# Gated recurrence and cosine MLP on one core: the evictions of a two-bank PSUM tile by two engines, without a wait between them

## The chip, the cores and the metric

The kernel runs on one core of a Trainium2 chip. A core has a matrix engine (TensorE: PE for the multiplications, PEld for its weight loads), three engines for elementwise work (VectorE or DVE, ScalarE or ACT, GpSimd or POOL), a sequencer that mostly issues DMAs (SyncE or SP), a memory of 128 partitions (SBUF), and an accumulator memory that TensorE writes (PSUM, eight banks for each partition; a bank holds 512 float32 values). Every engine works through its own queue of instructions in order; engines wait for one another by semaphores. The metric is the device time of one execution in microseconds (us), as the median of several runs.

## The reference

```
# q, k, v, alpha: (B, H, S, D) = (4, 8, 768, 48)
state = zeros(B, H, D, D)
for t in range(S):
    state = alpha[:, :, t, :, None] * state + einsum('bhd,bhe->bhde', k[:, :, t], v[:, :, t])
    y[:, :, t] = einsum('bhd,bhde->bhe', q[:, :, t], state)

x = y.transpose(0, 2, 1, 3).reshape(B * S, H * D)     # 3072 x 384
h = x @ w_in                                          # 384 -> 2048
out = (h * cos(h)) @ w_out                            # 2048 -> 384
```

A linear-attention recurrence with a decay for each channel is followed by an MLP whose activation is h cos(h). Inputs and output are float32.

## The kernel before

The 3072 tokens are cut into twelve steps J = 0 to 11, three for each batch entry; a step holds 256 tokens of all 8 heads, as two chunks c = 0 and 1 of 128 tokens. For each step the recurrence is computed in chunked form:

- `load` brings a (alpha), k, q and v into SBUF through SP's queue. `ln` takes the logarithm of a on ACT, `cums` sums it along the tokens by matmuls, `icp` and `exps` (on ACT) make the inverse and the plain cumulative products, and `scale_k` and `scale_q` (L212, L216; on POOL or DVE) multiply k and q by them into kh and qh. From J = 3 on POOL first multiplies pairs of a (`mul_a`, L149).
- `trans` (L260): 64 small transposes by PE write T_ps, a PSUM tile of two banks, one for each chunk c. `evict_T` (L266) copies bank c into half c of the SBUF tile qkT.
- `scores` (L274) computes A_ps of a chunk from qkT, `mask` (L279, DVE) masks it into A_sb.
- `outer` (L291) computes the chunk's state update U_ps; `add_state` (L305, L307, DVE) and `decay_state` (L313, POOL) carry the state un on.
- `yT` (L340) computes the recurrence's output y_ps, again a PSUM tile of two banks, one for each chunk. `evict_y` (L351) casts bank c into half c of the SBUF tile xT.
- The MLP: `mlp1` (L361) makes h_ps in four parts u, `cosine` (L367, ACT) makes c_sb, `gate` (L372, DVE) multiplies both into gsb, `mlp2` (L390, L384 for the last tile) makes o_ps in four parts for each chunk, `evict_o` (L402, L398) copies it out, `store` (L408) issues the DMA to HBM.

PSUM's eight banks are shared out: three two-bank buffers with the tag "h" go round among T_ps, A_ps, U_ps, y_ps, h_ps and a few smaller uses in the order in which they are asked for, one bank goes to o_ps, one to the cumulative sums. So whoever asks for an "h" buffer waits until the tile that used it three requests earlier has been read.

The order of all work is written out by hand: the table PLAN gives each step (such as `evT 0` of J = 3) a number, the steps are recorded in the order of these numbers, and each engine runs its share in that order. The numbers set an order only. A letter behind a number picks the engine: evictions of T go to DVE unless `:A` (ACT) stands there, evictions of y go to ACT unless `:D` (DVE) stands there. The rows that matter here:

```
"evT 0": "14773:A 18473:A 41585 48048 60976 71899 81566:A 93894 111044 116949:A 129834 138061",
"evT 1": "16453:A 19403:A 43330 48048:A 59896 72979 81586 93289 112124 117657 128759 137201:A",
"evy 0": "21333:D 27535:D 49128:D 60501:D 73683 92814:D 91919 110094:D 125423 140998 152879:D 163777:D",
"evy 1": "21333 27658 48990 59421:D 73683:D 92339:D 91549 110569:D 125793 141368 152128 163814",
```

The two halves of one tile are on different engines for T of J = 3, 6, 9 and 11 and for y of J = 0, 1, 2, 4, 10 and 11: ten pairs. The framework that places the waits treats the two-bank PSUM tile as one thing that two engines access, and makes the eviction that is recorded second wait for the first, although each reads a bank of its own and writes a half of its own. Whoever needs both halves then waits for the second alone.

Two more places are touched without a change in order: the last matmul of `yT` of J = 1 is remembered (GATES, AFTER), and the loads of a from J = 2 on, in SP's order, stand behind it; and `mlp2` counts which of its four parts is the first and the last of a tile.

Of the kernel before, what the change touches and what calls it, by code (L numbers as in the profile page):

```python
# [9 lines left out]
FP = mybir.dt.float32  # L10
# [6 lines left out]
def kernel(  # L17
# [10 lines left out]
    nc = tc.nc  # L28
    B, H, S, D = q.shape
    DM, DF = moe_w_in.shape  # L30
    C = 128
# [17 lines left out]
    ps = ctx.enter_context(tc.tile_pool(name="ps", bufs=1, space=bass.MemoryType.PSUM))  # L49
# [14 lines left out]
    for c in range(2):  # L64
        r = slice(HC * c, HC * c + HC)
# [105 lines left out]
    def two_banks(name):  # L171
        return ps.tile([C, 2, 512], FP, tag="h", name=name, bufs=3)
# [76 lines left out]
        )  # L249

    T_ps, A_ps, y_ps, U_ps = {}, {}, {}, {}

    def trans(J):
        T_ps[J] = ps.tile([C, 2, 2 * NP, 2, HC], BF, tag="h", name="T_ps", bufs=3)
        for i, x in ((1, kh_t[J % NQ]), (0, qh_t[J % NQ])):
            for p in range(NP):
                for e in range(2):
                    for c in range(2):
                        r = slice(HC * c, HC * c + HC)
                        nc.tensor.transpose(T_ps[J][:, c, i * NP + p, e, :],  # L260
                                            x[r, e, 2 * p : 2 * p + 2, :].rearrange("s h d -> s (h d)"), ident_bf[r, r])

    def evict_T(J, c, copy):
        if J not in qkT_sb:
            qkT_sb[J] = sb.tile([C, 2, 2 * NP, C], BF, tag="qkT", name="qkT", bufs=BUF["qkT"])
        copy(out=qkT_sb[J][:, c], in_=T_ps[J][:, c].rearrange("r n e s -> r n (e s)"))  # L266

    def scores(J, c):
        qkT = qkT_sb[J]
        A_ps[J, c] = ps.tile([C, 2, NP, C], FP, tag="h", name="A_ps", bufs=3)  # L270
        for p in range(NP):
            for a in range(2):
                r = slice(64 * a, 64 * a + D)
                nc.tensor.matmul(A_ps[J, c][:, a, p, :], qkT[r, c, NP + p, :], qkT[r, c, p, :], start=True, stop=True)  # L274

    def mask(J, c):
        if J not in A_sb:
# [39 lines left out]
    def yT(J):  # L317
        y_ps[J] = two_banks("y_ps")
        qkT, A, vs = qkT_sb.pop(J), A_sb.pop(J), vs_t[J % NS]
        todo = []  # L320
        for i in range(KT):
            for c in range(2):
                for g in range(4):
                    p, x = (4 * i + g) // 3, (4 * i + g) % 3
                    if (2 * J + c) % (2 * NJB) > 0:
                        U = U_new[2 * J + c - 1].rearrange("r p a d -> r p (a d)")
                        todo.append((c, g, i, U[:, p, 32 * x : 32 * x + 32], qkT[:, c, p, :]))
        for i in range(KT):
            for c in range(2):
                vf = vs[:, c].rearrange("s h d -> s (h d)")  # L330
                for half in range(2):
                    for g in range(4):
                        p, x = (4 * i + g) // 3, (4 * i + g) % 3
                        parts = {0: [(0, 0)], 1: [(0, 32), (1, 48)], 2: [(1, 80)]}[x]
                        for a, d in parts[half : half + 1]:
                            todo.append((c, g, i, vf[:, 128 * p + d : 128 * p + d + 32], A[:, c, a, p, :]))
        outs = [m[:3] for m in todo]
        begun = set()
        for z, (c, g, i, l, r) in enumerate(todo):
            last = nc.tensor.matmul(y_ps[J][32 * g : 32 * g + 32, c, i * C : (i + 1) * C], l, r,  # L340
                             start=(c, g) not in begun, stop=(c, g, i) not in outs[z + 1 :], skip_group_check=True)
            begun.add((c, g))
        for key, step in GATES.items():
            if step == ("yT", J):
                AFTER[key] = last

    def evict_y(J, c, copy):
        if J not in xT:
            xT[J] = sb.tile([C, KT, T2], BF, tag="xT", name="xT", bufs=BUF["xT"])

        copy(out=xT[J][:, :, c * C : (c + 1) * C].rearrange("r i (t e) -> r i e t", e=2),  # L351
             in_=y_ps[J][:, c, 0 : KT * C].rearrange("r (i e t) -> r i e t", i=KT, e=2))

    h_ps, c_sb, o_ps, o_sb = {}, {}, {}, {}

# [18 lines left out]

    HALVES = [slice(0, DM // 2), slice(DM // 2, DM)]

    def mlp2(J, c, part):
        if (J, c) == (NJ - 1, 1):
            if part == 0:

                o_ps[J, c] = [ps.tile([C, 512], FP, tag="x", name="o_last", bufs=1), two_banks("o_last")[:, 0]]
            for z, cols in enumerate(HALVES):
                for ft in range(part * NF // MP, (part + 1) * NF // MP):
                    nc.tensor.matmul(o_ps[J, c][z][:, 0 : DM // 2], gsb[J][:, ft, c * C : (c + 1) * C], w2[:, ft, cols],  # L384
                                     start=(ft == 0), stop=(ft == NF - 1))
            return
        if part == 0:
            o_ps[J, c] = ps.tile([C, 512], FP, tag="o", name="o_ps", bufs=1)
        for ft in range(part * NF // MP, (part + 1) * NF // MP):
            nc.tensor.matmul(o_ps[J, c][:, 0:DM], gsb[J][:, ft, c * C : (c + 1) * C], w2[:, ft],  # L390
                             start=(ft == 0), stop=(ft == NF - 1))

    def evict_o(J, c, copy):
        if (J, c) == (NJ - 1, 1):
            o_sb[J, c] = []
            for z, cp in enumerate((nc.scalar.copy, nc.vector.tensor_copy)):
                t = sb.tile([C, DM // 2], FP, tag=f"o_half{z}", name="o_half", bufs=1)
                cp(out=t, in_=o_ps[J, c][z][:, 0 : DM // 2])  # L398
                o_sb[J, c].append((t, HALVES[z], (nc.scalar, nc.sync)[z]))
        else:  # L400
            t = sb.tile([C, DM], FP, tag="o_sb", name="o_sb", bufs=4)
            copy(out=t, in_=o_ps.pop((J, c))[:, 0:DM])  # L402
            o_sb[J, c] = [(t, slice(0, DM), nc.sync)]

    def store(J, c):
# [6 lines left out]
    def idle(n):  # L412
# [132 lines left out]
```

## Time and profile before

| | |
|---|---|
| runs | 188.44 us median of 3 (188.35 to 189.09) |
| profiled execution: span from its first to its last instruction | 186.5 us |
| its own time | not given on the page; the median run lies 1.9 us over this span |
| PE busy | 176.7 us, 95% of the span |
| DVE, ACT, POOL busy | 135.4, 126.5 and 77.1 us |
| granted TensorE clock | 1.000 |
| input loads (k, a, v, q) | 12 of each, 384 KB each, a median of 6.0 to 6.3 us from issue to landing |
| HBM | read 25.17 MB, written 4.72 MB |

The profile is one execution, seen instruction by instruction. A row of the timeline has the start from the span's begin, the length, the engine, the line of the kernel, the operation with its output and inputs, the shapes, a count, and in brackets the idle time of the engine ahead of it with what ended it. Busy time is an average over stages: in the first 110 us the loads of q, k, v and a run beside the compute, after that nearly none. The list of waits sums, for each pair of waiter and releaser, the time in which an engine stood idle. Consecutive rows of one engine may overlap by some 0.1 us, since the next operation starts while the last one drains.

### The profile page before, as it was taken

To read this page: it belongs to the slowest core of one execution; us is meant where nothing else is said; L and a number is where in the kernel's file an instruction comes from. 1 tells how busy PE (TensorE), PEld (TensorE's weight loads), DVE (VectorE), ACT (ScalarE), POOL (GpSimd) and SP (SyncE) were. 2 spreads that over 40 slices of the span, in tenths; PEclk is the share of its full clock that TensorE was granted. 3 is DMA by queue.
4 is the path that set the end of the run, shared out by engine and by line. 5 is a ranking of instruction groups with operands and counts; after the bars stand their busy time and mean duration, and the time that the engine had idled before them with its cause. 6 is when DMAs were issued, how large, how long until landed. Compare 5 with 4: busy or idle time off the path is not lost.

```text
span 186.5 us, 5746 instructions
## 1 busy us (share of the span) xinstructions
PE 176.7 (95%) x2467; PEld 126.4 (68%) x2469; DVE 135.4 (73%) x184; ACT 126.5 (68%) x161; POOL 77.1 (41%) x110
## 2 busy tenths in 40 slices
PE   7988799989989999999999999999999999999993
PEld 2434588655667786785688668676867686786872
DVE  7178775589799979698847987794977556754461
ACT  2466876889498986889668999728965264373330
POOL 5079510257645653781896076930360320100000
PEclk9999999999999999999999999999999999999999
DMA  6999999999949979996799932600041005301102
GB/s 152 261 258 165 181 204 237 259 266 265 274 105 304 264 180 245 264 260 167 186 278 278 247 104 46 182 0 4 4 136 47 5 0 158 118 0 66 64 0 84
DMA packets 60137, 29.47 MB, mean 158 GB/s; under 512 B 51024, under 2 KB 60112, under 8 KB 60112
## 3 DMA queue, kind: packets, MB, share of 16 engines
q1 hardware_dynamic: 56256, 25.86, 57.2%
q0 software_dynamic: 3712, 3.15, 11.0%
q8 instruction: 19, 0.31, 0.7%
q10 hardware_dynamic: 144, 0.10, 0.2%
q14 instruction: 6, 0.05, 0.1%
HBM read 25.17 MB, written 4.72 MB: 160 GB/s over the span
## 4 chain that ended last, share of the span: by engine, by line
PE 73%; ACT 15%; DVE 8%; issue 3%; DVEq 0%
PE h_ps L361 31%; PE o_ps L390 24%; PE idle_ps L416 4%; PE y_ps L340 3%; ACT qkT L266 3%; DVE gsb L372 3%; PE T_ps L260 2%; ACT c_sb L367 2%; PE A_ps L274 2%; ACT L136 2%; ACT cp L200 2%; PE U_ps L291 2%; DVE kh L212 2%; ACT icp L192 2%; PE o_last L384 1%
## 5 line engine op out<-in xcount | busy, mean ns | idle before, releaser
L372 DVE TENSOR_TENSOR gsb<-h_ps,c_sb 128x1024 bf16<-128x1024 f32 x48 | 58.1, 1221 | 21.9 <-ACT c_sb L367 21.2
L367 ACT ACTIVATE c_sb<-h_ps,halfpi 128x1024 bf16<-128x1024 f32 x48 | 53.0, 1113 | 26.8 <-PE h_ps L361 23.0
L361 PE MATMUL h_ps<-xT,w 128*128 128x256 bf16 x576 | 66.7, 273 | 1.3 <-ACT xT L351 0.7
L390 PE MATMUL o_ps<-w,gsb 128*128 128x384 bf16 x368 | 66.7, 327 | 0.1
L361 PEld LDWEIGHTS <-w 128*128 128x128 bf16 x576 | 55.6, 98 | 10.1 <-issue 1.6
L390 PEld LDWEIGHTS <-gsb 128*128 128x128 bf16 x368 | 33.8, 98 | 21.2 <-DVE gsb L372 0.6
L313 POOL TENSOR_TENSOR un<-us,c 128x384 bf16<-128x384 f32 x20 | 16.7, 835 | 40.7 <-DVE us L305 29.1
L279 DVE TENSOR_TENSOR A_sb<-A_ps,msk 128x1024 bf16<-128x1024 f32 x24 | 28.9, 1215 | 1.7 <-PE A_ps L274 1.7
L212 POOL TENSOR_TENSOR kh<-k,icp 128x384 bf16<-128x384 f32 x17 | 16.9, 999 | 9.2 <-ACT icp L192 7.8
L216 POOL TENSOR_TENSOR qh<-q,cp 128x384 bf16<-128x384 f32 x15 | 15.0, 1006 | 11.8 <-ACT cp L200 11.8
L149 POOL TENSOR_TENSOR a<-a 128x384 f32<-128x384 f32 x9 | 9.0, 1001 | 12.6 <-DMA a<-in_alpha_dram 12.6
L219 POOL CAST vp<-v 128x768 bf16<-128x768 f32 x12 | 10.1, 841 | 8.8 <-DMA v<-in_v_dram 7.7
L416 PE MATMUL idle_ps<-zeros 128*128 128x512 bf16 x38 | 12.0, 457 | 1.4 <-DVE zeros L52 1.2
L141 ACT ACTIVATE lna<-a 128x768 bf16<-128x768 f32 x12 | 10.2, 847 | 4.6 <-DMA a<-in_alpha_dram 4.6
L266 ACT COPY qkT<-T_ps 128x1024 bf16<-128x1024 bf16 x8 | 8.0, 1015 | 6.9 <-PE T_ps L260 4.4
L136 ACT ACT_TABLE_LOAD x9 | 11.5, 1283 | 0.9 <-PEq L529 0.7
L367 ACT ACT_TABLE_LOAD x9 | 11.5, 1283 | 0.2
L266 DVE COPY qkT<-T_ps 128x1024 bf16<-128x1024 bf16 x16 | 10.8, 678 | 1.1 <-ACT qkT L266 1.1
L305 DVE TENSOR_TENSOR us<-U_ps,un 128x384 f32<-128x384 f32 x16 | 8.7, 550 | 3.8 <-PE U_ps L291 2.8
L402 DVE COPY o_sb<-o_ps 128x384 f32<-128x384 f32 x12 | 6.6, 551 | 6.5 <-PE o_ps L390 6.5
L351 ACT CAST xT<-y_ps 128x384 bf16<-128x384 f32 x12 | 6.7, 594 | 5.6 <-PE y_ps L340 3.8
L351 DVE CAST xT<-y_ps 128x384 bf16<-128x384 f32 x12 | 6.8, 584 | 4.7 <-PE y_ps L340 2.9
(69 smaller groups left out, 159.1 us busy)
## 6 DMA issues: line engine op xcount, KB each, us to landing
k<-in_k_dram SPq DMA_DIRECT2D x12, 384.0 KB, 6.0
a<-in_alpha_dram SPq DMA_DIRECT2D x12, 384.0 KB, 6.1
v<-in_v_dram SPq DMA_DIRECT2D x12, 384.0 KB, 6.0
q<-in_q_dram SPq DMA_DIRECT2D x12, 384.0 KB, 6.3
out_dram<-o_sb SPq DMA_DIRECT2D x23, 192.0 KB, 2.6
vs<-vp SPq DMA_DIRECT2D x36, 64.0 KB, 2.1
w<-in_moe_w_out_dram POOLq DMA_DIRECT2D x4, 384.0 KB, 10.1
w<-in_moe_w_in_dram POOLq DMA_DIRECT2D x4, 384.0 KB, 7.3
```

The costliest lines, as they stand in the source:

```text
L136: nc.scalar.preload_act_table_set("natural_log_exp_and_others")
L212: eng.tensor_tensor(out=kh_t[J % NQ][:, e, :, 0:D], in0=kqv["k", J][:, :, e], in1=icp_, op=ALU.mult)
L216: eng.tensor_tensor(out=qh_t[J % NQ][:, e, :, 0:D], in0=kqv["q", J][:, :, e], in1=cp, op=ALU.mult)
L266: copy(out=qkT_sb[J][:, c], in_=T_ps[J][:, c].rearrange("r n e s -> r n (e s)"))
L279: nc.vector.tensor_tensor(out=A_sb[J][:, c].rearrange("s a p t -> s (a p) t"), in0=A_ps.pop((J, c)).rearrange("s a p t -> s (a p) t"), in1 ...
L313: nc.gpsimd.tensor_tensor(out=u, in0=U_sum.pop(n), in1=c2_sb[J][:, :, c].unsqueeze(3).to_broadcast([C, NP, 2, D]), op=ALU.mult)
L351: copy(out=xT[J][:, :, c * C : (c + 1) * C].rearrange("r i (t e) -> r i e t", e=2), in_=y_ps[J][:, c, 0 : KT * C].rearrange("r (i e t) -> ...
L361: nc.tensor.matmul(h_ps[J, u][:, f, :], w1[:, kk, ft * C : (ft + 1) * C], xT[J][:, kk, :], start=(kk == 0), stop=(kk == KT - 1))
L367: nc.scalar.activation(out=c_sb[J, u], in_=h_ps[J, u], func=AF.Sin, bias=halfpi, scale=1.0)
L372: nc.vector.tensor_tensor(out=gsb[J][:, u * FW : (u + 1) * FW], in0=h_ps.pop((J, u)), in1=c_sb.pop((J, u)), op=ALU.mult)
L390: nc.tensor.matmul(o_ps[J, c][:, 0:DM], gsb[J][:, ft, c * C : (c + 1) * C], w2[:, ft], start=(ft == 0), stop=(ft == NF - 1))
L416: nc.tensor.matmul(idle_ps[0], zeros[:, 0:C], zeros, start=True, stop=True)
```

## The change

The two evictions of a tile are declared independent where they are on different engines. `apart` remembers the last eviction of each tile and its engine; if the next one of the same tile is on another engine, it tells the framework that there is no dependency between the two. The dependencies of both on the matmuls that write the tile, and of later users on both, are kept. PLAN is as it was. The rest of the diff rearranges code: the remembering of a step's last matmul becomes a function (`pass_gate`) that `scores` calls too, with no gate set there, and `mlp2` counts its parts instead of going by their number; neither moves an instruction.

```diff
+    evicts = {}
+
+    def apart(key, copy, ins):
+        if key in evicts and evicts[key][0] != copy:
+            tc.declare_no_dep(ins.ins, evicts[key][1].ins, reason="two engines each evict a bank of their own")
+        evicts[key] = copy, ins
...
     def evict_T(J, c, copy):
...
-        copy(out=qkT_sb[J][:, c], in_=T_ps[J][:, c].rearrange("r n e s -> r n (e s)"))
+        ins = copy(out=qkT_sb[J][:, c], in_=T_ps[J][:, c].rearrange("r n e s -> r n (e s)"))
+        apart(("T", J), copy, ins)
...
     def evict_y(J, c, copy):
...
-        copy(out=xT[J][:, :, c * C : (c + 1) * C].rearrange("r i (t e) -> r i e t", e=2),
+        ins = copy(out=xT[J][:, :, c * C : (c + 1) * C].rearrange("r i (t e) -> r i e t", e=2),
              in_=y_ps[J][:, c, 0 : KT * C].rearrange("r (i e t) -> r i e t", i=KT, e=2))
+        apart(("y", J), copy, ins)
...
+    def pass_gate(step, last):
+        for key, gate in GATES.items():
+            if gate == step:
+                AFTER[key] = last
...
-        for key, step in GATES.items():
-            if step == ("yT", J):
-                AFTER[key] = last
+        pass_gate(("yT", J), last)
...
+        last_tile = (J, c) == (NJ - 1, 1)
+        done = parts_done[J, c] = parts_done.get((J, c), 0) + 1
+        if done == 1:
...
+                nc.tensor.matmul(o[:, 0 : cols.stop - cols.start], gsb[J][:, ft, c * C : (c + 1) * C], w2[:, ft, cols],
+                                 start=(done == 1 and ft == fts[0]), stop=(done == MP and ft == fts[-1]))
```

More of the change, by code (lines that the diff above doesn't have):

```diff
@@ L259, in trans @@
                         r = slice(HC * c, HC * c + HC)
-                        nc.tensor.transpose(T_ps[J][:, c, i * NP + p, e, :],
+                        last = nc.tensor.transpose(T_ps[J][:, c, i * NP + p, e, :],
                                             x[r, e, 2 * p : 2 * p + 2, :].rearrange("s h d -> s (h d)"), ident_bf[r, r])
@@ L273, in scores @@
                 r = slice(64 * a, 64 * a + D)
-                nc.tensor.matmul(A_ps[J, c][:, a, p, :], qkT[r, c, NP + p, :], qkT[r, c, p, :], start=True, stop=True)
+                last = nc.tensor.matmul(A_ps[J, c][:, a, p, :], qkT[r, c, NP + p, :], qkT[r, c, p, :], start=True, stop=True)
+        pass_gate(("scores", J, c), last)
     def mask(J, c):
@@ L375 @@
     HALVES = [slice(0, DM // 2), slice(DM // 2, DM)]
+    parts_done = {}
     def mlp2(J, c, part):
-        if (J, c) == (NJ - 1, 1):
-            if part == 0:
+        last_tile = (J, c) == (NJ - 1, 1)
+        done = parts_done[J, c] = parts_done.get((J, c), 0) + 1
+        if done == 1:
+            if last_tile:
                 o_ps[J, c] = [ps.tile([C, 512], FP, tag="x", name="o_last", bufs=1), two_banks("o_last")[:, 0]]
[L382 to L391, printed above, removed]
+            else:
+                o_ps[J, c] = [ps.tile([C, 512], FP, tag="o", name="o_ps", bufs=1)]
+        fts = range(part * NF // MP, (part + 1) * NF // MP)
+        for o, cols in zip(o_ps[J, c], HALVES if last_tile else [slice(0, DM)]):
+            for ft in fts:
+                nc.tensor.matmul(o[:, 0 : cols.stop - cols.start], gsb[J][:, ft, c * C : (c + 1) * C], w2[:, ft, cols],
+                                 start=(done == 1 and ft == fts[0]), stop=(done == MP and ft == fts[-1]))
     def evict_o(J, c, copy):
@@ L401, in evict_o @@
             t = sb.tile([C, DM], FP, tag="o_sb", name="o_sb", bufs=4)
-            copy(out=t, in_=o_ps.pop((J, c))[:, 0:DM])
+            copy(out=t, in_=o_ps.pop((J, c))[0][:, 0:DM])
             o_sb[J, c] = [(t, slice(0, DM), nc.sync)]
```

## The prediction

> **What bounds the kernel now.** I read the page's busy shares first, then the list of waits, then the timeline around every place where TensorE stood still.
>
> The busy shares, part 1 of the page:
>
> ```profile
> PE 176.7 (95%) x2467; PEld 126.4 (68%) x2469; DVE 135.4 (73%) x184; ACT 126.5 (68%) x161; POOL 77.1 (41%) x110
> ```
>
> PE is busy 176.7 of 186.5 us, so a gain can come only out of PE's standing time. The granted clock is 1.000 over the span. Going through the timeline of PE, the gaps after its first 21 us are 0.65 us (ending 22.20), 0.26 (27.44), 0.61 (41.66), 0.11 (49.15), 0.59 (52.07), 0.26 (77.09), 0.35 (86.94), 0.12 (99.39) and 0.30 (120.06): 3.25 us in all. The list of waits (who waited for whom: us in total, times, longest) shows the waits that the change is about:
>
> ```profile
> ACT qkT L266 <- DVE qkT L266: 2.4, 1, 2.4
> ACT xT L351 <- DVE xT L351: 1.8, 3, 0.8
> DVE xT L351 <- ACT xT L351: 1.8, 2, 1.1
> DVE qkT L266 <- ACT qkT L266: 1.1, 2, 0.9
> PE h_ps L361 <- ACT xT L351: 0.7, 1, 0.7
> PE U_ps L291 <- DVE xT L351: 0.6, 1, 0.6
> PE U_ps L291 <- DVE gsb L372: 0.4, 1, 0.4
> PE h_ps L361 <- DVE xT L351: 0.3, 1, 0.3
> ```
>
> The first four are one eviction waiting for the other of its pair: 7.1 us over eight pairs. The last four are PE's own, and each follows one of those. The timeline (start, length, in brackets the idle time before) joins them, place by place:
>
> ```profile
> 20.94 0.59 DVE L351 CAST xT<-y_ps 128x384 bf16<-128x384 f32 x1
> 21.56 0.59 ACT L351 CAST xT<-y_ps 128x384 bf16<-128x384 f32 x1 [0.83 <-DVE xT L351]
> 22.20 4.09 PE L361 MATMUL h_ps<-xT,w 128*128 128x256 bf16 x36 [0.65 <-ACT xT L351]
> 27.44 1.47 PE L361 MATMUL h_ps<-xT,w 128*128 128x256 bf16 x12 [0.26 <-DVE gsb L372]
> ...
> 49.17 0.68 DVE L266 COPY qkT<-T_ps 128x1024 bf16<-128x1024 bf16 x1
> 49.88 1.01 ACT L266 COPY qkT<-T_ps 128x1024 bf16<-128x1024 bf16 x1 [2.40 <-DVE qkT L266]
> 50.79 0.60 ACT L351 CAST xT<-y_ps 128x384 bf16<-128x384 f32 x1
> 51.42 0.59 DVE L351 CAST xT<-y_ps 128x384 bf16<-128x384 f32 x1 [1.11 <-ACT xT L351]
> 52.07 0.51 PE L291 MATMUL U_ps<-vp,kh 64*128 64x96 bf16 x16 [0.59 <-DVE xT L351]
> ...
> 76.45 0.59 DVE L351 CAST xT<-y_ps 128x384 bf16<-128x384 f32 x1 [0.66 <-ACT xT L351]
> ...
> 85.07 0.69 DVE L266 COPY qkT<-T_ps 128x1024 bf16<-128x1024 bf16 x1 [0.90 <-ACT qkT L266]
> ```
>
> **The change, part by part.** Set side by side, the two programs have the same compute and DMA instructions in the same order on all engines. What differs is waits: ten pairs split over two engines (y of J = 0, 1, 2, 4, 10, 11; T of J = 3, 6, 9, 11) lose the wait for each other, and whoever needed only the later of the two now waits for both. PE gets two more waiting instructions and ACT one.
>
> *y of J=0 (22 us).* ACT is free from 20.74 (its vs copy, 19.92 + 0.82), y_ps is complete at 20.88, so the ACT half runs at 20.9 to 21.5, beside DVE's, and PE's h_ps starts at 21.6 to 21.7 instead of 22.20. Late next: DVE. c_sb would end 24.3 instead of 24.82, but DVE's us (24.04, waiting for POOL) ends 24.60, and DVE's next operation starts some 0.08 before the end of the one ahead, as 27.31 after 27.39 does. So the first gsb runs 24.52 to 25.74, the second 25.66 to 26.89 (it ended 27.39), and it frees the buffer of the h_ps that now starts 26.93 instead of 27.44. Gain 0.51, taken as 0.50; bounds 0.3 (only the move of the first gsb, 24.86 to 24.52) and 0.61 (all that PE gets at 22.20).
>
> *y of J=1.* PE has other h_ps work until 29.2 and the later half ends 28.51: nothing. If that cover were gone, ACT's idle 0.47.
>
> *T of J=3 and y of J=2 (49 to 52 us).* T_ps is written at 48.87 (48.47 + 0.40); ACT has been idle since 47.5, so its qkT half runs at 48.9 to 49.9. y_ps is complete at 50.06: ACT's xT half runs 50.1 to 50.7, DVE's after its cp (49.77 + 0.55) at 50.3 to 50.9. Scores and o_ps keep PE until 51.48, and U_ps, which waited for y_ps's buffer, starts there: 0.59 gained, all of the gap. Late next: the mask of A_ps, which frees the next h_ps buffer; it moves from 51.90 to 50.9 and stays ahead. Bounds 0.4 and 0.59.
>
> *y of J=4 (77 us).* DVE's half can start at 75.8 (its qkT ends 75.78, y_ps is complete at 75.74), ACT's ends 76.42, both ahead of PE's free time at 76.83: 0.26 gained.
>
> *T of J=6 (87 us).* DVE's qkT half starts at 84.1 (its gsb ends 84.17, T_ps is written at 83.98) and not 85.07, so the gsb behind it ends some 0.8 earlier than 86.89 and PE's 0.35 before U_ps goes.
>
> *T of J=9, 11, y of J=10, 11.* PE runs without a gap behind each of them (120.06 to the end), the engines' own idle time there is 0.18, 0, 0 and 0.48: nothing. They would be worth that much if PE were not the bound.
>
> *Costs.* A waiting instruction is 51 ns on PE's load side (the one row at L361); two, and ACT's, make at most 0.12; they stand where PE waits or has work queued: 0. In four places a weight load now carries a wait that only its matmul had; a load is 98 ns, and in none of them is the wait the last to end: 0, at most 0.4.
> Two evictions of one tile at the same time are not in this trace. Nearest rows: DVE's 16 qkT copies take 659 to 692 ns and ACT's 8 take 1012 to 1032, whatever ran beside them; ACT's copy at 140.49 took 1.01 while DVE's A_sb, from 140.72, read other PSUM. I take 0; the other end, one after the other as now, takes the whole gain away.
>
> *Sum:* 0.50 + 0.59 + 0.26 + 0.35 = 1.70 us off the span of 186.5. The runs' median is 188.44, 1.9 over that span, so I take the profiled execution as a median one and leave the 1.9: 186.7. The gains add up, because the gaps that stay between the places move with them: at 41.66 PE waits for DVE's qh, DVE (its kh at 39.16) for ACT's icp, ACT (37.88) for PE's cums; at 49.15 for POOL's un behind that same DVE; at 120.06 for DVE's gsb behind ACT's c_sb, which waited for PE (101.55). Between them PE has no gap, and a of J=2, which cums needs, lands at 34.3 for its use at 35.96, so 0.5 fits.
>
> **The rivals.**
> *More: a collision dissolves (186.1).* DVE's products of two SBUF tiles take 0.55 alone, but the second qh of J=2 took 1.35 (40.25 to 41.60), beside POOL's product on a (40.16 to 41.18, released by a load), and PE's 0.61 gap at 41.66 waits for it. DVE arrives 0.5 earlier at 39.74; POOL's load, behind a gate in yT of J=1 that moves by some 0.4, lands for 39.74 too. If DVE is first, the product is 0.55 and the gap goes: 1.70 + 0.61 = 2.31.
> [...]
>
> *Less: loads hold the first stage (187.2).* a of J=4 lands at 40.1 and v of J=2 at 41.6, both used within 0.1; if they don't move, the first 0.50 is lost. Against it: their queue is fed behind the gate that moves.
>
> *None: ACT holds (188.4).* From 102.9 to 119.6 ACT runs without a gap (table loads, c_sb, exponentials). If its start there didn't follow PE, the whole 1.70 would vanish in front of it. Against it: its c_sb at 98.65 and 101.55 each waited 0.20 for PE.
>
> *The waits remain by another way (188.4):* through a buffer's release or an engine's order. Against it: the wait lists name PE where they named the other evictor.
>
> *Slower: more collisions (190.4).* Seven DVE products (39.16 to 68.2 us: 0.69, 0.55, 1.35, 1.27, 0.55, 0.55, 0.79) would cost 3.70 more if every one met POOL and took 1.35; DVE is busy 11.15 of 11.40 us from 39.0 to 50.4, so it would pass to PE: 188.44 - 1.70 + 3.70. It decides from 2.64 us on (1.70 plus the 0.94 of 0.5%). Against it: POOL's work there waits on the same chain and moves with it.
>
> **How the numbers follow.** Forecast 0.50; more 0.18; loads 0.14; ACT 0.10; waits remain 0.04; slower 0.04. About 0.5% (0.94 us) is what a measurement of this kernel can tell from no change. Faster: 0.50 + 0.18 + 0.14 = 0.82; same 0.10 + 0.04 = 0.14; slower 0.04. The range runs from the larger gain (186.1, a little under for its 0.1 bounds) through 187.2 with the lower bounds 0.3 and 0.4 at their places and the uncovered 0.4 of weight loads: 186.0 to 187.8. It leaves out 0.18.
>
> **What would show it.** The list of waits no longer has any of its first four lines above. PE's gaps ending 22.20, 52.07, 77.09 and 86.94 are gone, with PE's gap near 27 at about 0.16; U_ps of J=3 stands 1.1 earlier, the T_ps at 120.06 stands 1.70 earlier, and PE's busy time stays 176.7. The forecast is wrong if evictions side by side take over 0.7 (DVE) or 1.05 (ACT), if the gap before T_ps at 41.66 closes or grows, or if a new PE gap stands between 27 and 49 or 102 and 120.

## The result and the profile after

The changed kernel takes 186.47 us (median of 4 runs, 185.82 to 186.89), the kernel before beside it on the same chip 188.45 us (188.35 to 189.09). The ratio is 0.9887 (95% interval 0.9859 to 0.9915): 1.6 to 2.7 us faster, most likely 2.0 to 2.1. The forecast was 186.7 us, 1.74 below the median of before.

The busy shares of the changed kernel:

```profile
PE 175.6 (95%) x2469; PEld 125.7 (68%) x2469; DVE 134.7 (73%) x184; ACT 126.4 (69%) x161; POOL 77.3 (42%) x110
```

The span went from 186.5 to 184.0 us in the profiled runs, with PE still 95% busy. (The profiled run of the changed kernel is its fastest, 185.82 us; what the run itself adds to the difference is told below.) The list of waits (waiter, line, releaser: us in total, times, longest) no longer holds any of the four lines in which one eviction waits for the other. In after, `evict_T` is L278, `evict_y` L363, `outer` L305, `mlp1` L374, `gate` L385. What evictions wait for now is PE, and PE's own waits have other names:

```profile
ACT qkT L278 <- PE T_ps L272: 5.8, 4, 2.2
ACT xT L363 <- PE y_ps L354: 4.0, 5, 1.6
DVE xT L363 <- PE y_ps L354: 3.2, 3, 2.3
PE cums L160 <- ACT lna L146: 0.4, 1, 0.4
PE T_ps L272 <- DVE gsb L385: 0.3, 1, 0.3
PE h_ps L374 <- DVE us L319: 0.3, 1, 0.3
PE U_ps L305 <- POOL un L327: 0.2, 1, 0.2
```

The timeline of the changed kernel at the four places of the forecast (start, length, engine, line, operation; in brackets the idle time before):

```profile
20.98 0.59 ACT L363 CAST xT<-y_ps 128x384 bf16<-128x384 f32 x1 [0.20 <-PE y_ps L354]
20.98 0.59 DVE L363 CAST xT<-y_ps 128x384 bf16<-128x384 f32 x1
21.72 2.78 PE L374 MATMUL h_ps<-xT,w 128*128 128x256 bf16 x24
23.23 0.83 POOL L327 TENSOR_TENSOR un<-us,c 128x384 bf16<-128x384 f32 x1 [2.00 <-DVE us L319]
24.09 0.56 DVE L319 TENSOR_TENSOR us<-U_ps,un 128x384 f32<-128x384 f32 x1 [0.95 <-POOL un L327]
24.79 1.47 PE L374 MATMUL h_ps<-xT,w 128*128 128x256 bf16 x12 [0.29 <-DVE us L319]
27.09 1.16 PE L374 MATMUL h_ps<-xT,w 128*128 128x256 bf16 x9
...
48.57 1.01 ACT L278 COPY qkT<-T_ps 128x1024 bf16<-128x1024 bf16 x1 [1.43 <-PE T_ps L272]
48.63 0.67 DVE L278 COPY qkT<-T_ps 128x1024 bf16<-128x1024 bf16 x1
49.59 0.59 ACT L363 CAST xT<-y_ps 128x384 bf16<-128x384 f32 x1
49.69 0.57 DVE L363 CAST xT<-y_ps 128x384 bf16<-128x384 f32 x1
50.77 0.51 PE L305 MATMUL U_ps<-vp,kh 64*128 64x96 bf16 x16
...
74.56 0.60 ACT L363 CAST xT<-y_ps 128x384 bf16<-128x384 f32 x1
74.56 0.59 DVE L363 CAST xT<-y_ps 128x384 bf16<-128x384 f32 x1
75.41 1.47 PE L374 MATMUL h_ps<-xT,w 128*128 128x256 bf16 x12
...
82.34 1.01 ACT L278 COPY qkT<-T_ps 128x1024 bf16<-128x1024 bf16 x1
82.40 0.68 DVE L278 COPY qkT<-T_ps 128x1024 bf16<-128x1024 bf16 x1
84.74 0.51 PE L305 MATMUL U_ps<-vp,kh 64*128 64x96 bf16 x16
```

Each pair now runs side by side, and neither engine is slowed: 0.67 and 0.68 us for DVE's qkT copy beside ACT's, 0.57 to 0.59 for its cast, 1.01 and 0.59 for ACT's, as before. The gaps in brackets in front of h_ps at 22.20, U_ps at 52.07, h_ps at 77.09 and U_ps at 86.94 are gone. One new gap stands in the first place, 0.29 at 24.79.

Where the time went is read by matching each PE instruction with itself in the other trace. The shift of its start (after less before) changes by 0.1 us or more at these instructions:

| before, us | after, us | shift, us | instruction, and what it waited for |
|---|---|---|---|
| 22.20 | 21.72 | -0.48 | h_ps of J=0: no longer for the later eviction |
| 24.82 | 24.79 | -0.03 | its third part: new gap, for DVE's us |
| 27.44 | 27.09 | -0.35 | its fourth part: no longer for DVE's gsb |
| 41.66 | 40.54 | -1.12 | T_ps of J=2: no longer for DVE's second qh |
| 44.40 | 43.64 | -0.75 | U_ps: new gap, for POOL's un |
| 46.47 | 46.13 | -0.34 | cums: new gap, for ACT's lna |
| 49.15 | 48.60 | -0.55 | y_ps of J=2: no longer for POOL's un |
| 52.07 | 50.77 | -1.30 | U_ps of J=3: no longer for the later eviction |
| 77.09 | 75.41 | -1.68 | h_ps: no longer for the later eviction |
| 86.94 | 84.74 | -2.20 | U_ps of J=6: no longer for DVE's gsb |
| 99.39 | 97.03 | -2.36 | h_ps: stands for "issue" 0.16 shorter than before |
| 177.98 | 175.51 | -2.47 | o_ps of J=11, after two small steps |

So by 87 us the change is worth 2.20 us: 0.35 in the first place, 0.20 at 49 us, 0.75 at U_ps of J = 3, 0.41 and 0.52 at the last two, less 0.03 between. Of the other 0.27 us, 0.16 is the shorter stop for "issue", which is not the change's, as the experiments show. The 0.11 behind it comes mainly in two small steps, 0.03 at 122.53 us of before (U_ps) and 0.06 at 177.98, which again and loads_late have as well.

### The profile page after: what moved, and what is told of

Same layout as the page of the kernel before. It is cut to its first block, busy times and chain, and to the rows that moved or that the text cites. A ratio compares the mean times of both kernels' runs of the same rounds, so it can differ in the third digit from the quotient of the medians.

```text
span 184.0 us, 5751 instructions
## 1 busy us (share of the span) xinstructions
PE 175.6 (95%) x2469; PEld 125.7 (68%) x2469; DVE 134.7 (73%) x184; ACT 126.4 (69%) x161; POOL 77.3 (42%) x110
## 3 DMA queue, kind: packets, MB, share of 16 engines
q0 software_dynamic: 3712, 3.15, 11.2%
## 4 chain that ended last, share of the span: by engine, by line
PE 73%; ACT 16%; DVE 3%; DMA 3%; issue 2%; SPq 1%; POOL 0%
PE h_ps L374 30%; PE o_ps L403 26%; PE y_ps L354 5%; DMA a<-in_alpha_dram 3%; ACT c_sb L380 3%; PE T_ps L272 3%; PE A_ps L287 3%; ACT L141 3%; ACT lna L146 3%; ACT cp L205 2%; ACT L380 2%; ACT qkT L278 2%; PE U_ps L305 2%; ACT icp L197 2%; PE o_last L403 1%
## 5 line engine op out<-in xcount | busy, mean ns | idle before, releaser
L385 DVE TENSOR_TENSOR gsb<-h_ps,c_sb 128x1024 bf16<-128x1024 f32 x48 | 58.0, 1220 | 21.8 <-ACT c_sb L380 21.2
L374 PE MATMUL h_ps<-xT,w 128*128 128x256 bf16 x576 | 66.8, 273 | 0.4 <-DVE us L319 0.3
L374 PEld LDWEIGHTS <-w 128*128 128x128 bf16 x576 | 55.4, 98 | 9.4 <-issue 0.8
L403 PEld LDWEIGHTS <-gsb 128*128 128x128 bf16 x400 | 36.4, 98 | 21.4 <-DVE gsb L385 0.4
L429 PE MATMUL idle_ps<-zeros 128*128 128x512 bf16 x40 | 11.5, 429 | 1.2 <-DVE halfpi L77 1.2
L278 ACT COPY qkT<-T_ps 128x1024 bf16<-128x1024 bf16 x8 | 8.0, 1015 | 5.9 <-PE T_ps L272 5.8
L278 DVE COPY qkT<-T_ps 128x1024 bf16<-128x1024 bf16 x16 | 10.7, 675 | 0.0
L287 PE MATMUL A_ps<-qkT 48*128 48x128 bf16 x192 | 9.2, 218 | 1.0 <-ACT vs L244 0.6
L287 PEld LDWEIGHTS <-qkT 48*128 48x128 bf16 x192 | 5.8, 94 | 5.5 <-issue 3.1
```

The costliest lines, as they stand in the source:

```text
L278: ins = copy(out=qkT_sb[J][:, c], in_=T_ps[J][:, c].rearrange("r n e s -> r n (e s)"))
L287: last = nc.tensor.matmul(A_ps[J, c][:, a, p, :], qkT[r, c, NP + p, :], qkT[r, c, p, :], start=True, stop=True)
L374: nc.tensor.matmul(h_ps[J, u][:, f, :], w1[:, kk, ft * C : (ft + 1) * C], xT[J][:, kk, :], start=(kk == 0), stop=(kk == KT - 1))
L385: nc.vector.tensor_tensor(out=gsb[J][:, u * FW : (u + 1) * FW], in0=h_ps.pop((J, u)), in1=c_sb.pop((J, u)), op=ALU.mult)
L403: nc.tensor.matmul(o[:, 0 : cols.stop - cols.start], gsb[J][:, ft, c * C : (c + 1) * C], w2[:, ft, cols], start=(done == 1 and ft == fts[0 ...
```

## The experiments

Three questions were open. Does each part pay what its place shows? Why did the runs of the changed kernel stand in two groups (185.8 to 186.1 and 186.9)? And was the collision at 40 us, which did dissolve, worth anything? Expectations that speak of theory C mean that DVE's collision with POOL, falling one way or the other, makes the two groups; theory F is that PE's instruction stream does.

**The same kernel again (again).** No edit.

> The changed kernel as it is, for more of its times. Its four times lie in two pairs, 185.82 and 186.06, 186.88 and 186.89; the profiled one (185.82) had the second qh of J=2 at 0.55 us where it took 1.35 before. Theory C (collision): which of DVE's qh and POOL's product on a of J=4 starts first is a matter of some 0.1 us, and it makes the two groups; expected here: two groups again, about 186.0 and 186.9, and a profile of a run near 186.9 has a qh of 1.35 and a gap before the second half of T_ps of J=2, while one near 186.0 has 0.55 and no gap. Rival P (places alone): the two groups are chance; a profile near 186.9 then has 0.55 too.

Measured: 186.15 us (186.00 to 186.81), ratio 0.9888 (0.9869 to 0.9907) to the kernel before, 188.44 beside it. The second qh again took 0.55 us, the trace behind the start follows that of after up to 97 us, and there a gap for "issue" of 0.24 us stands where after has none. The end is 0.28 later than in after, and the time 186.12 against 185.82.

**Only the T pairs, only the y pairs (t_only, y_only).** `apart` is limited to one kind:

```diff
-        if key in evicts and evicts[key][0] != copy:
+        if key in [("T", J) for J in (3, 6, 9, 11)] and key in evicts and evicts[key][0] != copy:
```

```diff
-        if key in evicts and evicts[key][0] != copy:
+        if key in [("y", J) for J in (0, 1, 2, 4, 10, 11)] and key in evicts and evicts[key][0] != copy:
```

> Only the T pairs (J = 3, 6, 9, 11) are freed, the y pairs still wait. Places: PE's gap at 52 us goes although y of J=2 still has its wait, since ACT's xT half starts at 50.1 instead of 50.8 and DVE's ends 51.3, when PE is free: 0.6 to 0.75 us; the gap at 87 goes, 0.35 as its length says or 0.51 if a gap also hides the 0.16 by which a matmul starts ahead of its predecessor's end. Sum 0.95 (gaps as they stand) to 1.25 (with the 0.16 each), so 187.5 or 187.2 beside 188.45. Theory C: nothing moves ahead of 48 us, so the second qh of J=2 stays at 1.35 and there is one group of times, as before. A rival by which the gain comes from the y pairs alone gives 188.4.

> Only the y pairs (J = 0, 1, 2, 4, 10, 11) are freed, the T pairs still wait. Places: 0.35 at 22 to 27 us, where DVE's sum of the state frees the next buffer; 0.6 at 52 us (the ACT half of T of J=3 ends at 50.9, ACT's xT at 51.4); 0.26 to 0.42 at 77; the gap at 87 stays. Sum 1.2 to 1.4, so 187.1 to 187.2. The two halves of the change then add to more than the whole, by the 0.6 at 52 us that either one gives. Theory C: as the first place moves DVE's qh ahead, this kernel has the coin of the changed one and two groups of times about 0.9 apart, 186.3 and 187.2; by the rival one group.

Measured: t_only 187.08 us, ratio 0.9934 (0.9916 to 0.9952); y_only 187.63, ratio 0.9957 (0.9938 to 0.9975). T alone gave a little more than expected (187.2 to 187.5), y alone 0.4 to 0.5 us less (187.1 to 187.2 was expected). In the trace T alone is worth 0.66 us at U_ps of J = 3 and 0.53 at U_ps of J = 6; the collision at 40 us dissolved in this run too, though nothing ahead of it is changed, which is taken up below. y alone is worth 0.37 in the first place, 0.62 at U_ps of J = 3 and 0.41 at 77 us, but part is paid back behind J = 3. The timeline of y_only:

```profile
49.32 1.01 ACT L278 COPY qkT<-T_ps 128x1024 bf16<-128x1024 bf16 x1 [2.20 <-DVE qkT L278]
53.14 1.28 ACT L380 ACT_TABLE_LOAD   x1
54.43 3.12 ACT L380 ACTIVATE c_sb<-h_ps,halfpi 128x1024 bf16<-128x1024 f32 x3
56.86 0.83 PE L374 MATMUL h_ps<-xT,w 128*128 128x256 bf16 x6 [0.49 <-DVE gsb L385]
```

ACT's qkT half still waits for DVE's, everything in ACT's queue behind it is late, and c_sb, 5 us on, makes PE wait 0.49 us for gsb. Either part alone takes most of U_ps's gap (0.66 and 0.62 of 0.75): the two parts of that place overlap. T alone keeps its gain, since ACT's queue is early with it; y alone pays most of it back.

**POOL's product out of DVE's way (mula_late).** POOL's product on a of J = 4 goes from 40.5 to 43.4 us, behind POOL's un of J = 1 and clear of DVE's second qh (in the profiled run both qh together took 1.01 us, from 39.68, and POOL's product 0.99).

```diff
-        "mula": "- - - 36680 41180 47582 54280 61956 76220 87867 79850 105765",
+        "mula": "- - - 36680 42700 47582 54280 61956 76220 87867 79850 105765",
-        "state 1": "18654 43450 - 61176 78120 - 96057 115635 - 131261 146038 -",
+        "state 1": "18654 42690 - 61176 78120 - 96057 115635 - 131261 146038 -",
```

> The changed kernel with POOL's product on a of J=4 moved behind its cast of v of J=2 and its un of J=1, so that it starts near 43.6 us instead of 40.5 and can't meet DVE's qh of J=2; kh of J=3 on POOL starts 0.3 later. Theory C: the second qh takes 0.55 in every run, the two groups become one at the faster level, 185.8 to 186.2. Rival P: the groups have another cause and stay, about 186.0 and 186.9, or the new order costs its 0.3 on top.

Measured: 186.42 us (186.24, 186.36, 186.42, 186.75, 186.75), ratio 0.9893 (0.9876 to 0.9910). Half a microsecond of spread stays without the collision, which theory C, with one group at 185.8 to 186.2, did not allow. The profiled run (186.75) has the gap for "issue" at 97 us with 0.62 us.

**The mask ahead of the first sum (mask_first).** In the first place DVE's us was late because a mask (1.20 us at 21.48 in after) runs ahead of the first sum. `mask 1` of J = 1 is recorded behind it.

```diff
-        "mask 1": "17993 21808 46625 51218 62056 84155 88867 106682 120280 127619 136921 143106",
+        "mask 1": "17993 23000 46625 51218 62056 84155 88867 106682 120280 127619 136921 143106",
```

> The changed kernel with DVE's second mask of J=1 moved behind its sum of the state of J=1, c=0 (the mask ran 21.4 to 22.6, the sum behind it). Theory: the first place gave 0.35 and not 0.50 because h_ps at 24.79 waited for the buffer of U_ps, freed by DVE's second sum at 24.60, which waits for POOL's un behind the first sum; now the first sum runs at 21.6, un at 22.2 to 23.0, the second sum ends at 23.8: the gap of 0.29 before 24.79 goes and h_ps at 27.09 moves to 26.85, 0.24 less in the whole if nothing later takes it, so about 185.9 for the faster group. Rival: the chain of ACT from 37 to 46 us takes it, and the time is that of the changed kernel, 186.1 with 186.8.

Measured: 186.95 us, ratio 0.9925 (0.9897 to 0.9952), 0.5 us above the changed kernel in the median (the intervals overlap) and far from the 185.9 that was expected. The timeline of PE in mask_first:

```profile
23.62 2.78 PE L374 MATMUL h_ps<-xT,w 128*128 128x256 bf16 x24 [0.36 <-DVE A_sb L293]
27.55 0.71 PE L374 MATMUL h_ps<-xT,w 128*128 128x256 bf16 x5 [0.26 <-DVE gsb L385]
...
41.77 0.41 PE L272 MATMUL T_ps<-ident_bf,qh 64*128 64x64 bf16 x16 [0.62 <-DVE qh L221]
...
46.57 0.32 PE L160 MATMUL cums<-lna,tri 128*128 128x384 bf16 x1
```

PE's wait for us is gone, but the mask frees a buffer too (that of A_ps), and h_ps waits for that one step earlier. In either order the DVE operation that stands second frees a buffer that PE needs sooner (0.29 us of waiting for us in after, 0.36 for the mask here). The run also answers the third question. With DVE 0.46 us later the collision is back (T_ps 1.23 us later than in after), and yet at 46.57 PE is only 0.44 behind after, at y_ps near 49 us 0.64: the collision costs 0.2 us, not 0.61. The runs in which it dissolved agree: each of them gains about 0.2 us between 46 and 49 us, t_only included.

**Only the five pairs that paid (paid5).** Freed are y of J = 0, 2, 4 and T of J = 3, 6.

```diff
-        if key in evicts and evicts[key][0] != copy:
+        if key in [("y", 0), ("y", 2), ("y", 4), ("T", 3), ("T", 6)] and key in evicts and evicts[key][0] != copy:
```

> Only five of the ten pairs are freed: y of J = 0, 2, 4 and T of J = 3, 6. Theory: the other five (y of J = 1, 10, 11, T of J = 9, 11) are worth nothing, PE has other work there, so the time is that of the changed kernel, 186.0 to 186.8, ratio 0.989. A rival by which freed evictions help wherever they stand has 0.2 to 0.9 us more than that: the five waits are 0.47 + 0 + 0.48 + 0.18 + 0 long.

Measured: 186.53 us, ratio 0.9891 (0.9866 to 0.9915): the whole gain, as far as the times can tell. The trace follows that of after up to 97 us. The other five pairs (y of J = 1, 10, 11 and T of J = 9, 11) are worth nothing that the times could show. The traces show 0.1 us: the step of 0.03 us at 122.53 stands in t_only and that of 0.06 at 177.98 in y_only, and paid5 has neither.

**Loads after the stretch at 94 to 97 us (loads_late).** Five loads are issued later, in case they delay the packet of the instruction queue that is described below.

```diff
-        "load k": "750 2544 28555 37270 46270 52480 58570 69470 72470 85140 91627 113474",
-        "load q": "5250 6750 29125 38770 48970 56370 57870 60070 78470 84570 87104 96187",
-        "load v": "3750 8250 35770 41770 51910 61570 67906 73970 75470 85710 95267 96757",
+        "load k": "750 2544 28555 37270 46270 52480 58570 69470 72470 85140 98550 113474",
+        "load q": "5250 6750 29125 38770 48970 56370 57870 60070 78470 84570 98600 98700",
+        "load v": "3750 8250 35770 41770 51910 61570 67906 73970 75470 85710 98650 98750",
```

> The changed kernel with five input loads (k, q and v of J=10, q and v of J=11) moved in SP's order behind the vs copies of J=7, which SP issues near 103 us; before, three of them are in flight from 90 to 100 us. Theory F (instruction fetch): the gap before one and the same weight load of PE (number 1368, at 97 to 99 us) has 0 to 0.9 us in the traces so far, is larger the later the page of PE's instructions that was asked for at 94 to 97 us lands, and makes the groups of times; with fewer loads beside it the page lands earlier, the gap is below 0.1 in the profile, and the times form one group at 185.8 to 186.1. Rival D (the gap is PE's own, or comes from elsewhere): gap 0 to 0.9 as before, groups at 186.1 and 186.8. If the loads are needed sooner than they land, a wait of POOL for k of J=10 near 110 us shows it, up to 1 us.

Measured: 186.22 us, ratio 0.9884 (0.9862 to 0.9905), with a gap of 0.39 us. Other loads moved up into the stretch and the DMA engines stayed as busy (a share of 1.16 against 1.20 from 94 to 97 us; the share is the time of all packets over that of 16 engines, and passes 1 where packets overlap), so the run says nothing on whether loads delay the packet.

**The kernel before once more (before_again).** No edit.

> The kernel before, for a second profile. The kernel with the T pairs alone had DVE's second qh of J=2 at 0.55 us though nothing ahead of it had changed, so the collision is a toss and not the change's: expected 0.55 or 1.35 here, and in either case PE at the sums of J=4 (46.47 us) within 0.1, because ACT's logarithm of a of J=4 ends last there. The gap before weight load 1368 is 0.1 to 0.6.

Measured: 188.90 us, span 187.1. The collision is there again (both qh together 1.82 us, as in the first profile), and PE is at the sums of J = 4 within 0.01 us. Against the first profile of before, one thing differs behind the start: the gap for "issue", 0.69 instead of 0.12 us. Its row, then that of paid5, then that of y_only, each from the timeline of PE:

```profile
99.96 1.25 PE L361 MATMUL h_ps<-xT,w 128*128 128x256 bf16 x10 [0.69 <-issue]
```

```profile
97.61 2.56 PE L374 MATMUL h_ps<-xT,w 128*128 128x256 bf16 x22 [0.69 <-issue]
```

```profile
99.04 1.14 PE L374 MATMUL h_ps<-xT,w 128*128 128x256 bf16 x9 [0.91 <-issue]
```

Kernels before and after have it, so it isn't the change's. Two runs with an equal gap, paid5 and before_again, differ by 2.24 us behind the gap and by 2.26 us in time (186.64 and 188.90): this is the five pairs that paid alone, and it agrees with the 2.20 of the table.

**Eight idle matmuls fewer, eight more (fewer8, more8).** The kernel has matmuls on zeros early on (`IDLE`: place and number), whose result nobody reads. Nothing else is changed in what is computed. If the gap belongs to a place in PE's instruction stream, 16 instructions fewer ahead of it (a matmul is a weight load and a matmul) move it later in the work, 16 more earlier. (The eight that fewer8 leaves out run at 12.7 and 14.3 us in after; the 16.4 us of the expectation is the place of another group.)

```diff
-    IDLE = [(1501, 16), (7915, 1), (9416, 8), (12569, 4), (14554, 5), (16389, 3), (18254, 3)]
+    IDLE = [(1501, 16), (7915, 1), (9416, 8), (14554, 1), (16389, 3), (18254, 3)]
```

```diff
-        for _ in range(n):
-            nc.tensor.matmul(idle_ps[0], zeros[:, 0:C], zeros, start=True, stop=True)
+        for _ in range(abs(n)):
+            w = 512 if n > 0 else 32
+            nc.tensor.matmul(idle_ps[0][:, 0:w], zeros[:, 0:C], zeros[:, 0:w], start=True, stop=True)
-    IDLE = [(1501, 16), (7915, 1), (9416, 8), (12569, 4), (14554, 5), (16389, 3), (18254, 3)]
+    IDLE = [(1501, 16), (1502, -8), (7915, 1), (9416, 8), (12569, 4), (14554, 5), (16389, 3), (18254, 3)]
```

> The changed kernel without eight of PE's idle matmuls of the start (four at 12.7 us, four at 16.4 us), so that everything behind them stands 16 instructions earlier in PE's stream. Theory F (instruction fetch): the gap of 0 to 0.9 us belongs to an edge in PE's instruction stream and not to the work there; the edge now falls eight weight loads later in the work, where the page has had 8 x 0.109 = 0.87 us more to land, so the gap at 97 us is below 0.1 and the times are one group near 185.8. Rival W (the work): the gap stays before the same h_ps matmul with its 0 to 0.9, groups 186.1 and 186.8. If the idle matmuls were needed to keep PE quick, T_ps at 13.7 us takes longer and the time grows by up to 0.5.

> The changed kernel with eight tiny idle matmuls more (32 columns) behind the first sixteen, at 5 us, where PE waits or nearly waits for the logarithm: everything behind them stands 16 instructions later in PE's stream. Theory F: the edge falls eight weight loads earlier in the work, the page has 0.87 us less, so the gap is 0.9 to 1.8 us, eight matmuls earlier, and the time 186.7 to 187.6. Rival W: the gap stays where it is, and the time is that of the changed kernel, 186.1 to 186.8, up to 0.3 more for the start.

Measured: fewer8 187.12 us (185.51 to 188.02), ratio 0.9930 (0.9899 to 0.9961); more8 187.02 us (186.46 to 187.14), ratio 0.9925 (0.9903 to 0.9947). In fewer8 the gap is gone, as theory F says, but something larger is lost: 1.0 us by 22 us, and more near 40 us, where the collision is back. In the windows (PE busy, instructions, and so on; the granted clock is the number behind POOL's) 13 to 21 us of fewer8 and then of after read:

```profile
13.00:21.00 8.00, 5.60 (x81) 3.15 (x81) 5.34 (x8) 4.56 (x5) 7.97 (x11) 0.57 1.17 182
```

```profile
13.00:21.00 8.00, 6.80 (x157) 3.78 (x157) 6.54 (x9) 5.28 (x7) 7.96 (x11) 1.00 1.17 182
```

In this run, with fewer idle matmuls, PE was granted 0.57 of its clock there, and did half as many matmuls. The clock over the span is 0.98 to 0.99 in eight of the ten runs of fewer8; the two at 1.0 took 185.51 and 186.19. The profile of more8 was of its fastest run (186.46):

```profile
93.81 2.13 PE L374 MATMUL h_ps<-xT,w 128*128 128x256 bf16 x18
96.66 1.58 PE L374 MATMUL h_ps<-xT,w 128*128 128x256 bf16 x13 [0.73 <-issue]
```

In all ten traces with the idle matmuls unchanged, PE stands when it has done 1367 to 1369 weight loads (records can be missing). In more8 it is again 1368, which is eight matmuls earlier in the work: after 21 matmuls of this group of h_ps (the view above begins inside the group and shows 18 of them), where after, again and paid5 stand after 29. Theory F predicted that place; the 0.89 us that PE loses in this run is at the lower end of its 0.9 to 1.8.

**A hundred tiny ones (more100).** The first 16 idle matmuls become 6 of 512 columns, 100 of 32 and one of 512, 91 more in all, so that the place falls on other work.

```diff
-    IDLE = [(1501, 16), (7915, 1), (9416, 8), (12569, 4), (14554, 5), (16389, 3), (18254, 3)]
+    IDLE = [(1501, 6), (1502, -100), (1503, 1), (7915, 1), (9416, 8), (12569, 4), (14554, 5), (16389, 3), (18254, 3)]
```

> The changed kernel with PE's sixteen idle matmuls of the start replaced by six, a hundred tiny ones (32 columns) and one: 91 more, so that everything behind them stands 182 instructions later in PE's stream. By theory F the edge before weight load 1368 then falls 91 loads earlier in the work, into the y matmuls that end near 94 us, and the next edge 37 loads later than the old one, in h_ps at about 101 us, each with slow work ahead of it: no gap of PE's own above 0.1 between 85 and 105 us, one group of times at 185.8 to 186.1, 0.3 to 0.4 below the median of the changed kernel. By rival W the gap at 97 us stays with its 0 to 0.9. If the tiny matmuls keep PE's clock less warm than the full ones, or the start ends after 7.1 us, up to 0.5 is lost there.

Measured: 186.87 us (186.51 to 187.41), ratio 0.9921 (0.9902 to 0.9941). There is no gap for "issue" between 85 and 105 us, as theory F says. But the time missed the 185.8 to 186.1 that was expected. Against after, 0.66 us is lost at the start, where POOL's vp waits 1.2 us longer for its load of v, and 0.5 us near 82 us, where T_ps waits for POOL's qh. PE's row at the start:

```profile
12.67 0.52 PE L305 MATMUL U_ps<-vp,kh 64*128 64x96 bf16 x16 [1.47 <-POOL vp L224]
```

Why the load came later is open. No variant was shown to be faster than the changed kernel.

## What the gap for "issue" is

Part 3 of the page names a queue for it (packets, MB, share of 16 engines), here of after:

```profile
q8 instruction: 19, 0.31, 0.8%
```

19 packets of 16 KB for some 4,940 matmuls and weight loads: 260 instructions in each, if PE's are what they carry; more100, with 182 instructions more, has 20. In after the first starts when PE has done 91 weight loads, the last at 2374: 127 apart on average (the expectation of more100 takes 128). One of them travels between 94 and 98.4 us. In the traces, with the time that PE loses between two matmuls of h_ps beyond their usual 0.109 us:

| kernel | packet ends, us | PE goes on, us | between, us | PE lost, us |
|---|---|---|---|---|
| after | 95.50 | 96.92 | 1.42 | 0.13 |
| t_only | 96.89 | 98.17 | 1.28 | 0.24 |
| before | 97.99 | 99.39 | 1.40 | 0.28 |
| again | 95.72 | 97.19 | 1.47 | 0.41 |
| loads_late | 96.02 | 97.30 | 1.28 | 0.55 |
| mask_first | 96.61 | 98.10 | 1.49 | 0.67 |
| mula_late | 96.18 | 97.81 | 1.63 | 0.79 |
| paid5 | 96.02 | 97.61 | 1.59 | 0.85 |
| before_again | 98.39 | 99.96 | 1.57 | 0.86 |
| y_only | 97.70 | 99.04 | 1.34 | 1.07 |

PE goes on 1.28 to 1.63 us after the packet's end, whether it stood for 0.13 or 1.07 us. This is read as PE standing until a page of instructions is there; the traces show the times, not what a packet carries. More8 fits (its packet ends at 95.10 us, PE goes on 1.56 us later). The packet starts when PE is at its weight load 1345 to 1355, only 13 to 23 loads ahead of the place, and right ahead of it PE issues its instructions very densely: 100 matmuls of y_ps and 32 transposes in 2.1 us (91.53 to 93.61 in after). That PE uses up its page too soon for that reason is argued and not tried. Why the packet comes at other times in equal runs (94.27 to 94.82 in after, again and paid5) is open: the loads keep the DMA engines busy there (a share of 1.20 from 94 to 97 us in after), and no run unloaded them.

This makes the spread of the runs that could be compared. Over the profiled runs of after, again, loads_late and paid5, whose traces are alike up to 97 us, the loss goes 0.13, 0.41, 0.55, 0.85 and the time 185.82, 186.12, 186.23, 186.64. No run of the changed kernel near 186.9 was profiled, so that its upper group comes from the same stop isn't shown. A second, smaller difference stands at the start: from 8 us on PE's work is 0.12, 0.23 and 0.28 us later in mask_first, t_only and mula_late than in before, and at most 0.05 in the others of the table; its cause is open.

## Why the prediction was right, step by step

**The mechanism** was as told: evictions side by side at their old lengths, four waits gone, no cost for the added waits, and the other five pairs worth almost nothing (0.1 us in the traces). The four terms, 0.50 + 0.59 + 0.26 + 0.35 = 1.70, measured 0.35 + 0.75 + 0.41 + 0.52 = 2.03. With 0.20 from a place that had been given nothing, and 0.03 lost between the places, it is 2.20; with the 0.1 of the other five pairs it is 2.3. The median moved by 1.98 and, when the kernel was run again, by 2.29. So the sum was 0.6 too small, and that 186.7 lies 0.23 from the measured 186.47 is in part luck: equal runs of the changed kernel differ by 1 us.

**"Gain 0.51, taken as 0.50" in the first place was too high.** The step named DVE as late next and followed its gsb. It overlooked that DVE's us, which it had down as ending at 24.60, also frees U_ps's buffer for PE's third part of h_ps. In before PE came there only at 24.82, so the wait didn't show. With PE 0.48 earlier it shows as the 0.29 gap at 24.79, and the 0.48 shrinks to 0.03. The closed gap at 27.44 then gives 0.35, just above the lower bound of 0.3.

**"0.59 gained, all of the gap", "0.26 gained" and the "0.35" were too low, all by the same amount.** They measured 0.75, 0.41 and 0.52: 0.15 to 0.17 more. The length of a gap was taken for its price. 24 matmuls of h_ps take 2.78 us and 36 take 4.09, so one starts every 0.109 us while it is 0.273 long: a matmul that waits for nothing starts 0.16 before the end of the one ahead. A gap of 0.59 between an end and a start is a loss of 0.75. The bound "0.4 and 0.59" was therefore too tight above.

**Of the rivals**, the one with a dissolved collision came about, but not at its price. From the timelines of the changed kernel:

```profile
39.44 1.01 DVE L221 TENSOR_TENSOR qh<-q,cp 128x384 bf16<-128x384 f32 x2
40.49 1.00 POOL L154 TENSOR_TENSOR a<-a 128x384 f32<-128x384 f32 x1 [1.39 <-DMA a<-in_alpha_dram]
40.54 0.40 PE L272 MATMUL T_ps<-ident_bf,qh 64*128 64x64 bf16 x16
...
45.23 0.84 ACT L146 ACTIVATE lna<-a 128x768 bf16<-128x768 f32 x1
46.13 0.32 PE L160 MATMUL cums<-lna,tri 128*128 128x384 bf16 x1 [0.36 <-ACT lna L146]
```

DVE came first, two products took 1.01 us, and the gap of 0.61 in front of T_ps closed. But the rival's own account has a wrong step: "behind a gate in yT of J=1 that moves by some 0.4". SP issues the loads of a behind that gate at these times, in before and in after:

```profile
27.24 0.99 SPq L105 DMA_DIRECT2D a<-in_alpha_dram  x2
```

```profile
27.21 0.99 SPq L110 DMA_DIRECT2D a<-in_alpha_dram  x2
```

The gate moved by 0.03 us, because the new gap at 24.79 stands ahead of yT of J = 1 and the 0.35 is gained only behind it. So the loads didn't move with PE. POOL's product on a starts at 40.49 us in after and at 40.06 to 40.23 in again, paid5, loads_late and y_only, against 40.16 and 40.20 in the two profiles of before, while DVE's second qh starts 0.33 to 0.38 earlier than in before and is now first in all five. In t_only DVE is not earlier, and there it is first because the load came later (POOL at 40.72); what delayed it is open. That the product takes 0.55 if DVE is first was an assumption of the forecast, and the rows bear it out: with DVE first, both qh took 1.01 us in after; with POOL's product from 40.16 beside them, 1.82 in before. (What lengthens them, no trace shows.) But 5 us on, PE waits for ACT's lna, and there the shift is back at -0.34, all of it given back. ACT runs from 37.54 to 47.15 us without a gap, and from 37.88 to 47.5 in before: that stretch of ACT starts at PE's cums_h, moves by the 0.34 of the first place and by nothing else. The forecast had tested ACT for such a stretch only at 102.9 to 119.6. ACT's rows in the profile of before would have priced the rival at almost nothing. What is left, 0.2 at y_ps near 49 us, comes by DVE's us being earlier; it is missing in mask_first, in which the collision is back.

The rival "loads" was set aside because "their queue is fed behind the gate that moves"; the gate didn't move. Loads did take part of the gain for a moment (U_ps at 43.64 waits 0.23 us for POOL's un, which waits behind vp for v of J = 2), but nothing of the first place's. ACT's stretch from 102.9 on followed PE, since the shift of T_ps, 120.06 to 117.70, is kept. The waits didn't return by another way. The collisions that were to cost 3.70 didn't multiply: DVE's kh near 45 us went from 1.27 to 0.60 and qh behind it from 0.55 to 1.35, one for the other.

**Signs that were named in advance.** U_ps of J = 3 stands 1.30 us earlier (1.1 was said), T_ps at 120.06 2.36 (1.70 was said), of which 0.16 is the shorter stop for "issue". The gap of "about 0.16" that was to stay near 27 us is gone. Two signs of being wrong came true: the gap before T_ps at 41.66 closed, and new PE gaps stand between 27 and 49 us (0.23 at 43.64 and 0.36 at 46.13). So the step "the gaps that stay between the places move with them" was wrong here; the time holds nonetheless, because the one nearly pays for the other. PE's busy time "stays 176.7" and was 175.6. In traces of one and the same kernel it is 175.6 and 176.2, of before 176.7 and 176.1, and the idle matmuls of the start alone take 11.2 to 12.7 us in them, so that sign could not tell anything below 1 us.

## What to carry to other kernels

A gap that closes pays until the next engine without idle time: before a gap is counted, look on every engine between it and the next place for a stretch without idle time, and for the buffers that free PE's next tiles, for there an earlier start turned into a new wait (0.36 us for ACT's lna, 0.29 for DVE's us). Look also which side of a gate the gain falls on: here the loads behind it stayed where they were. On TensorE price a gap from start to start, not from end to start: here a matmul of h_ps that waits for nothing started 0.16 us before the end of the one ahead. Where equal runs differ by half a microsecond, compare their traces instruction by instruction before a cause is sought in the change.

## What was not expected of the hardware

- PE stood for "issue", 0.13 to 1.07 us, at the same place of its stream (1367 to 1369 weight loads done) in kernels before and after, and went on 1.28 to 1.63 us after a 16 KB packet of the instruction queue had ended. With eight more matmuls ahead (more8) it stood eight matmuls earlier in the work; with 91 more (more100, 182 instructions) there was no such gap between 85 and 105 us; that kernel lost time elsewhere (0.66 us at the start, 0.5 near 82 us).
- With eight idle matmuls fewer at 13 to 15 us the profiled run was granted a clock of 0.57 between 13 and 21 us instead of 1.00, eight of ten runs had less than 1.00 over the span, and the median was 0.65 us above that of the changed kernel.
- In after ACT and DVE read two banks of one PSUM tile at the same time, with PE at work on other tiles, and each kept its lengths to 0.02 us: qkT copies of 0.67 and 0.68 us on DVE (0.66 to 0.69 in before) beside 1.01 on ACT (1.01 to 1.03), xT casts of 0.57 to 0.59 on DVE (0.57 to 0.60) beside 0.59 and 0.60 on ACT (0.59 to 0.60).
